# TensorE's code as one loop over two buffers: keys, values and every weight in 20 rounds of the same matmuls

## The chip, the cores and the metric

The kernel runs on one core of a Trainium2 chip. The metric is the device time of one execution in microseconds (us). Before the change it is 777.16 us, the median of 3 runs (777.11 to 777.27).

## What is computed

One decode step of a gated mix of grouped-query attention and an MLP, all in float32, for B = 2 sequences of one token, D = 1024, 32 query heads, 4 key/value heads, a cache of 32768 positions with 128 numbers each, and an MLP width F = 3584:

```python
g = sigmoid((x * gate_w).sum(-1, keepdims=True))
q = (x @ wq)                                   # 32 heads x 128
a = softmax(q @ k.T * 128 ** -0.5) @ v @ wo    # 8 query heads for each key/value head
h2 = gelu(layernorm(x) @ w3) @ w4
out = g * a + (1 - g) * (x + h2)
```

The reference has a token-shift branch with w1 and w2 too. With one token each of its shifts pads the only position away, so it adds zeros, and neither kernel loads w1 or w2. Keys and values are 2 x 134 MB, wq and wo 16.8 MB each, w3 and w4 14.7 MB each: 331 MB are read once, each used for two rows (weights) or eight query rows (caches).

## The kernel before

**Buffers and loads.** Two buffers, buf0 and buf1, each 128 partitions x 16384 numbers (8 MB), take turns. All large loads are issued by SyncE (SP) on one DMA queue: wq in two loads, w3 in two, w4 in two, then for each of the 8 pairs (key/value head x sequence) two loads of keys and two of values, then wo, whose second half comes in pieces of 8, 4, 2, 1 and 1 thousand columns (`PIECES`). A load into a buffer waits until TensorE's own count (class `Line`: one counter per engine, increased by marked instructions) says that the last matmul on the buffer's former contents is done. The small operand, x and gate_w as 16 rows of 192 numbers (x16, L140), comes first, on ScalarE's queue.

**TensorE (PE).** Its program is written out in full except for one loop. All its matmuls but one (L227) go through the helper at L135, and waits of the form "a count, then subtract it" through L132 (`take`).
- L167 to L178: x16 is spread over 128 partitions by matmuls with a selection matrix (spread), then come the sums for the gate and for the layer norm, and 16 matmuls that place the residual x(1-g) in acc, the PSUM bank that adds up the output to the end.
- L185 and L186 multiply x by wq (`columns`, L148), L187 to L194 transpose the result to queries (q_t); L195 to L204 do the same for w3 and the hidden row; L205 to L210 add h times w4 to acc (`into_acc`, L161).
- L213 to L274 are a loop (`t.Fori`) over the 8 pairs, one piece of code: 64 matmuls for scores, a transpose of the maximum (mt) and its broadcast back (bp), four times 16 small transposes of the exponentials (`turn`, L236), twice 32 matmuls with values (L245), the row sums (lp), and 8 matmuls that gather the heads (op).
- L280 to L291: the eight heads' results times wo into acc, load by load and piece by piece.

The weights of a matmul here are 32 columns wide, and four matmuls with 512 columns of the buffer fill the four quarters of 32 partitions of a PSUM bank. The scores of a pair stand in four banks (sc), 128 rows that are 8 heads x 16 slices of the cache.

**VectorE (DVE) and ScalarE (ACT)** are written out for all 8 pairs. DVE takes the maximum of the scores (L419 to L422), works out the bias (L429), copies transposed exponentials back (L435, L439) and scales the result (L456); ACT takes the exponentials (L432) and shares the copies (L437, L441). DVE's last instruction copies acc to o_sb (L464), which SP stores (L502). GpSimd (POOL) only fills constants and zeros at the start (L297 to L314).

Of the kernel before, what the change touches and what calls it, by code (L numbers as in the profile page):

```python
# [10 lines left out]
ALU = mybir.AluOpType  # L11
AX = mybir.AxisListType

# [8 lines left out]
KF = F // P  # L22
C = 32
G = P // C
# [4 lines left out]
KT = KF // G  # L29
STEP = C // B  # L30
PIECES = (8, 4, 2, 1, 1)


class Line:


    def __init__(self, engine, sem):
        self.engine, self.sem, self.n, self.seen = engine, sem, 0, {}

    def wait(self, line, value):  # L40
        if self.seen.get(id(line), 0) < value:
            self.seen[id(line)] = value
            self.engine.wait_ge(line.sem, value)

    def own(self):
        self.wait(self, self.n)

    def did(self, ins, to=None):
        if to is None:
            self.n += 1  # L50
            ins.then_inc(self.sem, 1)
        else:
            ins.then_inc(to, 1)
        return self.n
# [3 lines left out]
def kernel(  # L58
# [17 lines left out]
    def psum(name):  # L76
        return ctx.enter_context(nc.psum_tensor(name, [P, 512], F32))[:, :]
# [8 lines left out]
    bufs = [sbuf("buf0", RUN), sbuf("buf1", RUN)]  # L86
    ident = sbuf("ident", P)
    ones = sbuf("ones", P)
    spread = sbuf("spread", 4 * (P + 1), 16)
    place = sbuf("place", 3 * P + 2)  # L90
    x16 = sbuf("x16", KD * KD * 3, 16)
    xs = sbuf("xs", KD * 3)
    x_pad, xn_pad, xr_pad = (sbuf(n, KD * C) for n in ("x_pad", "xn_pad", "xr_pad"))
    h_pad = sbuf("h_pad", KF * C)
    o_pad = sbuf("o_pad", HQ * C)
    q_cur = sbuf("q_cur", E * E * C)
    sel = sbuf("sel", G * REP)
    sel_all = sbuf("sel_all", REP)
    xw, xc, sq = (sbuf(n, KD * B) for n in ("xw", "xc", "sq"))
# [3 lines left out]
    row = sbuf("row", 1024)  # L103
    q_t = sbuf("q_t", HQ * B * E)
    hid, cube, inner, bent = (sbuf(n, KT * E * PAIRS) for n in ("hid", "cube", "inner", "bent"))
    mx, l4 = ([sbuf(f"{n}{i}", NI) for i in range(2)] for n in ("mx", "l4"))
    m1, l1, bias = ([sbuf(f"{n}{i}", 1) for i in range(2)] for n in ("m1", "l1", "bias"))
    m8, mb = sbuf("m8", REP, 1), sbuf("mb", P, 1)
    lsel, norm, factor = (sbuf(n, REP) for n in ("lsel", "norm", "factor"))
    p_sb = [sbuf(f"p{i}", 512) for i in range(NI)]  # L110
    p_t = [sbuf(f"pt{i}", 512) for i in range(NI)]
    pv_sb = sbuf("pv_sb", E * 512)
    o_sb = sbuf("o_sb", D // G)
    sc = [psum(f"sc{i}") for i in range(NI)]
    tr = [psum("tr0"), psum("tr1")]
    pv = psum("pv")
    acc_bank = psum("acc")
    acc = acc_bank[:, :D // G]
    compact = at(ident, 0, (STEP, PAIRS))

    with tc.tile_critical(sync_engine=mybir.EngineType.Pool, no_gpsimd_drain=True):
        new = tc.alloc_semaphore
        landed = [new("landed0"), new("landed1")]
        pieces = [landed[1]] + [new(f"piece{i}") for i in range(1, len(PIECES))]
        edge, dvp, acp = new("edge"), new("dve_to_pe"), new("act_to_pe")
        dve, act = Line(nc.vector, new("dve")), Line(nc.scalar, new("act"))
        pool, sp = Line(nc.gpsimd, new("pool")), Line(nc.sync, None)
        pe = Line(nc.tensor, new("pe"))
        v, s, t = nc.vector, nc.scalar, nc.tensor

        def take(sem, n=1):
            t.wait_ge(sem, n).then_inc(sem, -n)  # L132

        def mm(o, lhsT, rhs, start, stop):
            return t.matmul(o, lhsT, rhs, start=start, stop=stop, skip_group_check=True)  # L135

        def quarter(t_, g):
            return t_[C * g:C * g + C]

        nc.scalar.dma_start(x16, xg.rearrange("(j p) k c -> j (p k c)", j=16)).then_inc(edge, 16)  # L140


        events = {}

        def mark(name, ins):
            events[name] = pe.did(ins)

        def columns(load, pad, n, banks):  # L148
            wide = n // G
            take(landed[load % 2], 16)  # L150
            for ek in range(E * E):
                for u, bank in enumerate(banks):
                    lo, hi = u * 512, min(u * 512 + 512, wide)
                    for g in range(G):
                        start = ek * n + g * wide
                        last = mm(quarter(bank, g)[:, :hi - lo], at(pad, ((load % 2) * 4 + ek) * C, (1, C)),
                                  bufs[load % 2][:, start + lo:start + hi],
                                  load % 2 == 0 and ek == 0, load % 2 == 1 and ek == 3)
            mark(f"load{load}", last)

        def into_acc(lhsT, rows, stop=False):  # L161
            for g in range(G):
                last = mm(quarter(acc, g), lhsT, rows[:, g * (D // G):(g + 1) * (D // G)], False, stop)
            return last
# [112 lines left out]
        def at_pair(m, name):  # L277
            return events[name] + m * per_pair
# [256 lines left out]
```

## Time and profile before

| | |
|---|---|
| median of 3 runs | 777.16 us |
| the profiled execution | 777.0 us |
| its span | 775.2 us |
| TensorE busy | 424.1 us (55%) |
| VectorE busy | 71.5 us (9%) |
| ScalarE busy | 37.2 us (5%) |
| GpSimd busy | 4.1 us (1%) |
| mean granted TensorE clock | 0.771 |
| read from memory | 331.36 MB, 427 GB/s over the span |

The profile is one execution. Its span runs from the first to the last recorded event; 1.8 us of the execution lie around it. In the profile page the digits of a row such as "DMA" are the busy share of 40 equal slices of the span, in tenths. In the table of DMA queues, q1 is SP's queue with the large loads and the store, q10 ScalarE's queue with x16, and the "instruction" queues bring the engines' own code (q8 TensorE's, q14 the others'); the columns are packets, megabytes, and the time that the packets took as a share of 16 DMA engines over the stretch. A row of the list of DMA issues gives the median time from a load's issue to its landing. A row of the timeline reads: start in us, busy time, engine, line, operation, output<-inputs, shapes, the count of instructions drawn together, and in brackets the idle time before and who ended it. A row of the groups reads: shape and count | total busy us, mean ns of one | idle time before and who ended it. "PEq L132" stands for TensorE's sequencer at a `take`. A row of the windows reads: the stretch, its length, then the busy time of PE, its weight loads, DVE, ACT, POOL and SP (the last as 0), the granted TensorE clock, the share of time in which the DMA engines are busy, and GB/s.

### The profile page before, as it was taken

The page shows a single profiled execution, that of the slowest core. Times are in us where ns is not written, and L with a number is a line of the kernel's source. Part 1 is how long each engine was busy: PE and PEld are TensorE (multiplying, and loading weights), DVE is VectorE, ACT ScalarE, POOL GpSimd, SP SyncE. Part 2 cuts the span into 40 slices and gives each one's busy share as a digit, 9 for nine tenths or more (in the row PEclk, how much of TensorE's full clock was granted, in tenths as well). Part 3 has the DMA queues.
Part 4 walks back from the last instruction along what each step waited for, and adds up shares of the span by engine and source line. Part 5 has one row for each costly group of instructions (what it writes and reads, how often), then busy time and mean ns, then how long its engine had stood idle before and what let it go on. Part 6 is the DMA issues. An engine that isn't in the chain of part 4 may idle for free. (4 is left out here: it accounts for less than half of the span.)

```text
span 775.2 us, 8891 instructions
## 1 busy us (share of the span) xinstructions
PE 424.1 (55%) x4148; PEld 181.4 (23%) x4148; DVE 71.5 (9%) x203; ACT 37.2 (5%) x88; POOL 4.1 (1%) x14
## 2 busy tenths in 40 slices
PE   3454654573647354845573647354845573647355
PEld 2121231141213121412141213121412141213123
DVE  3000100020002000200020002000200020102000
ACT  1000100020002000200020002000200020002000
POOL 2000000000000000000000000000000000000000
PEclk9876666796779776867796779777867796779779
DMA  9999999999999999999999999999999999999996
GB/s 379 437 432 454 433 418 434 433 435 434 436 433 436 433 436 436 433 433 433 433 430 433 433 433 433 433 433 436 433 433 433 433 433 433 433 433 433 433 422 263
DMA packets 6397, 331.56 MB, mean 428 GB/s; under 512 B 728, under 2 KB 752, under 8 KB 1008
## 3 DMA queue, kind: packets, MB, share of 16 engines
q1 hardware_dynamic: 6352, 331.36, 99.0%
q8 instruction: 10, 0.16, 0.1%
q14 instruction: 3, 0.02, 0.0%
q10 hardware_dynamic: 32, 0.01, 0.0%
HBM read 331.36 MB, written 0.01 MB: 427 GB/s over the span
## 5 line engine op out<-in xcount | busy, mean ns | idle before, releaser
L135 PE MATMUL sc<-buf,q_cur 128*32 128x512 f32 x1024 | 147.5, 740 | 135.9 <-PEq L132 135.9
L135 PE MATMUL pv<-buf,pt 128*32 128x512 f32 x1024 | 130.5, 668 | 106.1 <-PEq L132 106.1
L135 PEld LDWEIGHTS sc<-buf,q_cur 128*32 128x32 f32 x1024 | 40.4, 133 | 236.8 <-issue 236.8
L135 PEld LDWEIGHTS pv<-buf,pt 128*32 128x32 f32 x1024 | 38.5, 121 | 185.3 <-issue 185.1
L419 DVE TENSOR_REDUCE mx<-sc 128x1 f32<-128x512 f32 x32 | 22.1, 692 | 293.4 <-PE sc L135 293.4
L432 ACT ACTIVATE p<-sc,bias 128x512 f32<-128x512 f32 x32 | 21.6, 685 | 563.0 <-DVE bias L429 563.0
L135 PE MATMUL tr<-ident,p 128*64 128x64 f32 x1024 | 42.4, 260 | 9.2 <-PEq L132 9.2
L135 PEld LDWEIGHTS tr<-ident,p 128*64 128x64 f32 x1024 | 41.5, 172 | 9.8 <-issue 9.7
L452 DVE COPY pv_sb<-pv 128x512 f32<-128x512 f32 x16 | 10.3, 686 | 164.9 <-PE pv L135 164.9
L135 PE MATMUL sc<-buf,x_pad 128*32 128x512 f32 x128 | 16.4, 670 | 15.2 <-PEq L132 15.2
L135 PE MATMUL acc<-buf,h_pad 128*32 128x256 f32 x224 | 16.9, 474 | 14.1 <-PEq L132 14.1
L135 PE MATMUL sc<-buf,xn_pad 128*32 128x384 f32 (+1 forms) x128 | 16.6, 683 | 13.7 <-PEq L132 13.7
L135 PE MATMUL tr<-sel,pv_sb 128*128 128x8 f32 x128 | 17.3, 271 | 12.0 <-PEq L132 12.0
L135 PE MATMUL acc<-buf,o_pad 128*32 128x256 f32 x256 | 17.2, 420 | 11.9 <-PEq L132 11.9
L135 PEld LDWEIGHTS tr<-sel,pv_sb 128*128 128x128 f32 x128 | 16.8, 212 | 19.0 <-issue 19.0
L135 PEld LDWEIGHTS acc<-buf,h_pad 128*32 128x32 f32 x224 | 9.3, 136 | 21.3 <-issue 18.8
L135 PEld LDWEIGHTS acc<-buf,o_pad 128*32 128x32 f32 x256 | 9.5, 120 | 19.1 <-issue 16.2
L135 PEld LDWEIGHTS sc<-buf,x_pad 128*32 128x32 f32 x128 | 5.0, 122 | 26.2 <-issue 26.2
L135 PEld LDWEIGHTS sc<-buf,xn_pad 128*32 128x32 f32 x128 | 5.2, 135 | 24.5 <-issue 24.5
L135 PE MATMUL tr<-x,spread 16*128 16x24 f32 x16 | 3.6, 384 | 8.5 <-DMA x<-xg 8.5
L447 DVE RECIPROCAL norm<-tr 128x8 f32<-128x8 f32 x8 | 1.7, 208 | 67.2 <-PE tr L135 67.2
L435 DVE COPY pt<-tr 128x512 f32<-128x512 f32 x8 | 5.5, 692 | 19.0 <-PE tr L135 19.0
(78 smaller groups left out, 98.3 us busy)
## 6 DMA issues: line engine op xcount, KB each, us to landing
buf<-w SPq DMA_DIRECT2D x4, 7168.0 KB, 25.3
buf<-wo SPq DMA_DIRECT2D x1, 4096.0 KB, 21.3
buf<-wo SPq DMA_DIRECT2D x1, 2048.0 KB, 25.9
buf<-wo SPq DMA_DIRECT2D x1, 1024.0 KB, 28.3
buf<-wo SPq DMA_DIRECT2D x2, 512.0 KB, 29.5
buf<-kt SPq DMA_DIRECT2D x16, 29.9
buf<-vt SPq DMA_DIRECT2D x16, 29.3
buf<-wq SPq DMA_DIRECT2D x2, 32.0
```

Of the source, the lines that this page charges most:

```text
L135: return t.matmul(o, lhsT, rhs, start=start, stop=stop, skip_group_check=True)
L419: dve.did(v.reduce_max(out=mx[i2][:, i:i + 1], in_=sc[i], axis=AX.X))
L432: act.did(s.activation(p_sb[i], sc[i], AF.Exp, bias=bias[i2], scale=scale, accum_out=l4[i2][:, i:i + 1]), acp)
L435: dve.did(v.tensor_copy(p_t[0], tr[0]), dvp)
L447: dve.did(v.reciprocal(norm, tr[0][:, :REP]))
L452: dve.did(v.tensor_copy(at(pv_sb, e * P, (E * P, G), (H, 2), (1, H)), at(pv, e, (P, G), (0, 2), (2, H))), dvp if e else None)
```

## The change

TensorE's whole program becomes one loop of two phases (L185), so that its longest part is written once. Phase 0 (the Else branch, L188, which stands last) is two sums for the gate and the layer norm; phase 1 is `rounds()` (L136): 20 rounds, each of which multiplies one load in buf_a and one in buf_b by 32 column blocks of weights (`sets`, L122). In a round all 32 groups of buffer x stand in two PSUM banks; a piece that only odd rounds need (the maximum, its broadcast, the row sums, the gathering of heads) stands in an `If`. What differs between wq, w3, keys, values, w4 and wo is only what DVE, ACT and POOL write into the weights wt_a and wt_b and how they read the PSUM banks. Code with registers and branches replaces written-out code on ACT, DVE and POOL too: each has its own loop over the 8 pairs (L217, L477, L268).

- **Loads.** buf_a gets wq, wq, then all keys in turn, then wo twice; buf_b gets w3, w3, the first half of w4, then all values, and at the end the second half of w4 in pieces of 6, 4, 2, 1 and 1. SP alternates between the two, and waits for one counter `go` that DVE raises (`free`) when it has seen TensorE's event.
- **x.** One load on ScalarE's queue brings x and gate_w as 2 x 64 rows of 48 numbers (x2, L195): its source pattern has an outer dimension of 2 with step 0, so both halves of the partitions get the same 64 rows. DVE picks from it what each half needs (xs), so the spreading matmuls are gone. ScalarE's sigmoid now comes ahead of its square root.
- **Scores and exponentials.** DVE copies the scores to s_sb, which frees the PSUM banks for the next round; ACT writes each block of exponentials twice, in two layouts (`spread_rows`, p_dup); TensorE turns them with eight matmuls of 128 columns by a permutation (perm) in place of 64 small transposes, twice a round in a loop (L157); DVE copies them into wt_b (`turned`). The queries and the weight rows for wo are copied into wt_a by POOL (`queries`, `heads`).
- **End.** The residual x(1-g) enters as 4 groups of columns of a constant part of buf_b in the w3 rounds. The product with wo and with the first part of w4 gathers in acc_sb on DVE (`masked`), and four matmuls add it to acc before the last piece (L172).

```diff
+def sets(x, which, event=False):
+    for n4 in which:
+        for g in range(G):
+            n, bank = n4 * G + g, n4 // 2 % 2
+            last = mm(ps[x][C * g:C * g + C, bank * 512:bank * 512 + 512],
+                      wt[x][:, n * C:n * C + C], buf[x][:, n * 512:n * 512 + 512],
+                      n4 in (0, 2), n4 in (3, 4, 5, 7))
...
+def rounds():
+    with t.Fori(0, ROUNDS) as i:
+        with t.If(i > 0):
+            sets(1, range(5, 8), True)
+            with odd(i):
...
+        take(t, landed[0], 16)
+        take(t, ready[0])
+        sets(0, range(8), True)
+        with t.If(i < ROUNDS - 1):
+            with odd(i):
...
+            with t.Fori(0, 2):
+                take(t, acp)
+                take(t, dvp)
+                for k in range(8):
+                    last = mm(tr[:, k * P:(k + 1) * P], p_dup[:, k * P:(k + 1) * P], perm)
+                last.then_inc(pd, 1)
+        take(t, landed[1], 16)
+        take(t, ready[1])
+        sets(1, range(3))
+        take(t, piece, 16)
+        sets(1, range(3, 5), True)
...
-nc.scalar.dma_start(x16, xg.rearrange("(j p) k c -> j (p k c)", j=16)).then_inc(edge, 16)
+s.dma_start(x2, bass.AP(xg.tensor, xg.offset, [[0, 2], [2 * KD * 3, H], [1, 2 * KD * 3]])
+            ).then_inc(edge, 16)
...
+with v.Fori(0, PAIRS) as m:
+    got()
+    free()
+    scores(1)
+    wait_order()
+    v.tensor_tensor(m1, mx[:, :1], mx[:, 1:], op=ALU.max).then_inc(dvp, 1)
+    keep(1)
...
-                sp.wait(pe, needs)
-            nc.sync.dma_start(bufs[i % 2][:, :n], src).then_inc(landed[i % 2], 16)
+                sy.wait_ge(go, j - 1)
+            sy.dma_start(buf[x][:, :src.shape[1]], src).then_inc(landed[x], 16)
```

TensorE's program before, from the matmuls of w4 through the loop over pairs (L213) to wo; a row is a run of like instructions as written, with the tile of the moving and of the stationary operand behind the arrow:

```order
L135 MATMUL acc<-buf,h_pad 32x256 x112
L213 UNCONDITIONAL_BRANCH
L135 MATMUL sc<-buf,q_cur 32x512 x64
L227 MATMUL tr<-ident,m 1x128
L135 MATMUL tr<-ones,mb 128x1
L135 MATMUL tr<-ident,p 64x64 x64
L135 MATMUL pv<-buf,pt 32x512 x32
L135 MATMUL tr<-lsel,ones 128x8
L135 MATMUL pv<-buf,pt 32x512 x32
L135 MATMUL tr<-sel,pv_sb 128x8 x8
L213 REGISTER_ALU
L213 COMPARE_AND_BRANCH
```

TensorE's program after, from the head of the round (L138 asks whether it is the first) through the matmuls of buf_a to those of buf_b and the branch back (L137):

```order
L138 COMPARE_AND_BRANCH
L119 MATMUL ps_b<-buf_b,wt_b 32x512 x12
L134 REGISTER_ALU
L134 COMPARE_AND_BRANCH
L119 MATMUL sm<-lsel,ones 128x8
L119 MATMUL sm<-sel_all,pv_t 128x8 x2
L140 UNCONDITIONAL_BRANCH
L119 MATMUL ps_a<-buf_a,wt_a 32x512 x32
L151 COMPARE_AND_BRANCH
```

```order
L119 MATMUL tr<-perm,p_dup 128x128 x8
L157 REGISTER_ALU
L157 COMPARE_AND_BRANCH
L151 UNCONDITIONAL_BRANCH
L119 MATMUL ps_b<-buf_b,wt_b 32x512 x20
L137 REGISTER_ALU
L137 COMPARE_AND_BRANCH
```

The keys' and the values' matmuls, which followed one another within a pair, are now two halves of a round, and the rows for wq, w3, w4 and wo have gone into the same two; as written, TensorE has 657 matmuls before and 99 after. The last of the round's matmuls on buf_b (12 of 32) stand at the head of the next round.

SP's program before, from its start (bufs are alternated; "waits pe" is the wait for TensorE's count):

```order
L475 DMA buf0<-wq 128x16384
L475 DMA buf1<-wq 128x16384
L475 DMA buf0<-w3 128x14336 [waits pe]
L475 DMA buf1<-w3 128x14336 [waits pe]
L475 DMA buf0<-w4 128x14336 [waits pe]
L475 DMA buf1<-w4 128x14336 [waits pe]
L475 DMA buf0<-kt 128x16384 [waits pe]
```

SP's program after, from its start ("waits dve_to_sp" is the wait for the counter `go`):

```order
L567 DMA buf_a<-wq 128x16384
L567 DMA buf_b<-w3 128x14336
L567 DMA buf_a<-wq 128x16384 [waits dve_to_sp]
L567 DMA buf_b<-w3 128x14336 [waits dve_to_sp]
L567 DMA buf_a<-kt 128x16384 [waits dve_to_sp]
L567 DMA buf_b<-w4 128x14336 [waits dve_to_sp]
L567 DMA buf_a<-kt 128x16384 [waits dve_to_sp]
L567 DMA buf_b<-vt 128x16384 [waits dve_to_sp]
```

Both issue two loads without a wait and every later one behind a wait. The second load is now w3's, the third is wq's second half, and the engine waited for is VectorE instead of TensorE; the number of loads and their bytes are the same.

ScalarE's program before, from its start, with the semaphores that it waits for:

```order
L140 DMA x<-xg 16x192
L140 UNCONDITIONAL_BRANCH
L355 ACT_TABLE_LOAD
L355 ACTIVATE dev<-var 128x2 [waits dve]
L357 ACT_TABLE_LOAD
L357 ACTIVATE gate<-tr 128x2 [waits pe]
```

ScalarE's program after, from its start:

```order
L195 DMA x<-xg 128x1x48
L198 ACT_TABLE_LOAD [waits dve_to_act]
L198 ACTIVATE gate<-sm 128x2
L200 ACT_TABLE_LOAD [waits dve_to_act]
L200 ACTIVATE dev<-var 128x2
```

The load of x is 128 rows of 48 numbers where it was 16 of 192, and the table loads stand behind the waits for DVE's results where they stood ahead of them.

More of the change, by code (lines that the diff above doesn't have):

```diff
@@ L12 @@
 AX = mybir.AxisListType
+POOL = mybir.EngineType.Pool
 P = 128
@@ L21 @@
 NT = 4
-KF = F // P
-C = 32
-G = P // C
 WIDE = 8192
@@ L370 @@
-        act.did(s.copy(row[:, 512:], sc[1]), acp)
-        dve.wait(pe, events["q"])
-        dve.did(v.tensor_copy(q_t, tr[1][:, :HQ * B * E]))
-        def queries(m):
-            dve.own()
-            for half, (lo, hi) in enumerate(halves):
-                for c in range(2):
-                    last = v.tensor_copy(
-                        at(q_cur, c * C + (2 * c + half) * REP, (2 * C, E), (1, REP), rows=(lo, hi)),
-                        at(q_t, m, (PAIRS, E), (E * PAIRS, REP), rows=(lo, hi)))
-                    dve.did(last, dvp if half and c else None)
```

783 lines of the change are left out of this document (414 added, 369 removed).

## The prediction

> **What bounds the kernel now.** I read the page first, then the timeline of TensorE and the DMA view of single stretches.
>
> ```profile
> span 775.2 us, 8891 instructions
> ...
> DMA  9999999999999999999999999999999999999996
> ...
> q1 hardware_dynamic: 6352, 331.36, 99.0%
> q8 instruction: 10, 0.16, 0.1%
> q14 instruction: 3, 0.02, 0.0%
> q10 hardware_dynamic: 32, 0.01, 0.0%
> ...
> buf<-kt SPq DMA_DIRECT2D x16, 29.9
> buf<-vt SPq DMA_DIRECT2D x16, 29.3
> ```
>
> The 16 DMA engines are busy from the first slice to the last. The queue q1 holds the weights and caches: 331.36 MB in 99.0% of 16 x 775.2 us is 27.0 KB per us and engine, so a row of 64 KB takes 2.43 us, and a load of 128 rows, 8 per engine, 19.4 us. A load lands 29.9 us after its issue, so it waited some 10 us in the queue: the queue never runs dry, and compute is covered by that much.
>
> The timeline shows it as a cadence. These are the starts of TensorE's work on a load (column 1; column 2 is its length), each set off by that load's landing, and the end of the program:
>
> ```profile
> 8.51 3.60 PE L135 MATMUL tr<-x,spread 16*128 16x24 f32 x16 [8.51 <-DMA x<-xg]
> ...
> 23.11 7.07 PE L135 MATMUL sc<-buf,x_pad 128*32 128x512 f32 x64 [1.92 <-PEq L132]
> ...
> 43.46 9.30 PE L135 MATMUL sc<-buf,x_pad 128*32 128x512 f32 x64 [13.28 <-PEq L132]
> ...
> 60.99 8.21 PE L135 MATMUL sc<-buf,xn_pad 128*32 128x512 f32 x64 [5.08 <-PEq L132]
> ...
> 77.78 8.36 PE L135 MATMUL sc<-buf,xn_pad 128*32 128x512 f32 x64 [8.57 <-PEq L132]
> ...
> 94.74 8.42 PE L135 MATMUL acc<-buf,h_pad 128*32 128x256 f32 x112 [5.57 <-PEq L132]
> ...
> 111.69 8.48 PE L135 MATMUL acc<-buf,h_pad 128*32 128x256 f32 x112 [8.53 <-PEq L132]
> ...
> 440.65 8.68 PE L135 MATMUL sc<-buf,q_cur 128*32 128x512 f32 x64 [5.46 <-PEq L132]
> ...
> 460.00 9.24 PE L135 MATMUL sc<-buf,q_cur 128*32 128x512 f32 x64 [10.67 <-PEq L132]
> ...
> 750.27 9.21 PE L135 MATMUL acc<-buf,o_pad 128*32 128x256 f32 x128 [7.32 <-PEq L132]
> ...
> 771.35 0.64 PE L135 MATMUL acc<-buf,o_pad 128*32 128x256 f32 x8 [0.59 <-PEq L132]
> 772.05 0.42 DVE L464 COPY o_sb<-acc 128x256 f32<-128x256 f32 x1 [28.87 <-PE acc L135]
> 772.50 0.69 SPq L502 DMA_DIRECT2D out<-o_sb  x1
> ```
>
> A full load takes 460.00 - 440.65 = 19.35 us, and the 33 from 111.69 to 750.27 take 19.35 each; w3 and w4, 7/8 as long, take 16.95. With no delay the last piece would be at 23.11 + 35 x 19.35 + 4 x 16.95 = 768.2, and 0.3 for the small pieces at the end (estimate): 768.5. It is at 771.35, so 2.9 us are lost, and the steps say where: 23.11 to 43.46 is 1.0 too long, 43.46 to 60.99 is 0.6, and 750.27 to 771.35 is 1.4. The stretches in which the code queue q8 had packets fit. Of the DMA view, 0 to 25, 25 to 120, 120 to 200 and 750 to 772 us in turn:
>
> ```profile
> q10 hardware_dynamic: 32, 0.01, 0.2%
> ...
> q8 instruction: 5, 0.08, 0.3%
> ...
> q8 instruction: 3, 0.05, 0.3%
> ...
> q8 instruction: 2, 0.03, 0.6%
> ```
>
> That is all ten; from 200 to 750, where TensorE runs its loop (L213) again and again, there is none. A packet is 16 KB and holds one engine for 0.3% of 16 x 95 us / 5 = 0.9 us (0.6% of 16 x 22 / 2 = 1.1). A landing waits for its last engine, and an engine that never idles carries its delay to the end. The last microseconds in windows (columns before the last: TensorE's clock and the DMA share) show how unevenly they finish:
>
> ```profile
> 766.00:767.00 1.00, 1.00 (x20) 0.75 (x24) 0.00 (x0) 0.00 (x0) 0.00 (x0) 1.00 0.95 377
> 767.00:768.00 1.00, 0.90 (x19) 0.32 (x8) 0.00 (x0) 0.00 (x0) 0.00 (x0) 1.00 0.81 328
> 768.00:769.00 1.00, 0.13 (x4) 0.16 (x8) 0.00 (x0) 0.00 (x0) 0.00 (x0) 1.00 0.48 197
> 769.00:770.00 1.00, 0.94 (x16) 0.34 (x11) 0.00 (x0) 0.00 (x0) 0.00 (x0) 1.00 0.13 53
> 770.00:771.00 1.00, 0.64 (x8) 0.19 (x8) 0.00 (x0) 0.00 (x0) 0.00 (x0) 1.00 0.07 29
> ```
>
> Their shares sum to 2.4 us, so the mean engine is done at 768.4, the last about 771.2.
>
> **The change part by part.** Bytes and the cadence stay, so 768.5 stays. *Code.* TensorE's 657 written matmuls needed 0.16 MB of fetched code, 245 bytes each; 99 need 24 KB, under two packets. One was there at the start (nothing was fetched before 25 us, some 50 matmuls into the program), so one fetch stays. It falls at the start, where the program jumps to its end; nothing is fetched in the last load. The one may hit the engine that ends last (1.0, the step from 23.11) or another (0): I take 0.9, so of 2.9 us 2.0 go. The other engines' three fetches of 8 KB (q14) stay as many: VectorE has as many instructions as before.
>
> *x.* 32 small packets took 0.2% of 16 x 25 us, 0.025 us each; 128 rows with their counters are some 144, 9 per engine: 0.2 us (0 to 0.4), if they spread over all engines.
>
> *The rounds.* What hides the rest is a round of two loads, 38.7 us. The durations, from the groups (mean ns behind the comma) and four rows of the timeline:
>
> ```profile
> L419 DVE TENSOR_REDUCE mx<-sc 128x1 f32<-128x512 f32 x32 | 22.1, 692 | 293.4 <-PE sc L135 293.4
> L432 ACT ACTIVATE p<-sc,bias 128x512 f32<-128x512 f32 x32 | 21.6, 685 | 563.0 <-DVE bias L429 563.0
> L435 DVE COPY pt<-tr 128x512 f32<-128x512 f32 x8 | 5.5, 692 | 19.0 <-PE tr L135 19.0
> L355 ACT ACT_TABLE_LOAD x1 | 1.3, 1283 | 1.3 <-PEq L528 1.3
> ...
> 479.35 7.07 PE L135 MATMUL pv<-buf,pt 128*32 128x512 f32 x64 [2.33 <-PEq L132]
> ...
> 432.62 2.57 PE L135 MATMUL tr<-sel,pv_sb 128*128 128x8 f32 x16 [1.50 <-PEq L132]
> ...
> 470.04 0.16 DVE L421 TENSOR_REDUCE m<-mx 128x1 f32<-128x4 f32 x1
> ...
> 471.71 0.16 DVE L429 COPY bias<-tr 128x1 f32<-128x1 f32 x1 [0.53 <-PE tr L135]
> ```
>
> In the longer (odd) round the keys land at 0, and TensorE, cold after its wait, is done at 9.3. VectorE then releases the buffer, before any other work on this result; SP, which waited for TensorE before, now waits for that, with all later loads behind it, so a VectorE that is behind would hold the DMA. At this point it has nothing else to do. The maximum over 1024 columns takes two of the 0.69 (10.7), the steps from it to the bias 1.8 as now, plus 1.4 for the copy of the scores that stands between them on VectorE (13.9). Two exponentials take 1.4 (15.5 with the hand-over). Eight matmuls with 128 weight columns took 2.57 at 8 moving columns; 128 moving columns add up to 7.07 / 8 / 4 = 0.22 each where nothing overlaps, so 2.6 to 4.4 (18 to 20). Then 1.4 for the next exponentials, beside VectorE's two copies of the first block, the second eight matmuls, and two copies: the weights for the values stand at 24 to 27. The values landed at 19.35. Their 32 matmuls come warm, 7.07: the buffer is free at 31 to 34. It has to be by 38.7 less 1 us of start-up (the first issue at 0.9, data from about 1.9) and 2 us by which the first engines lead, 35.5. The even round lacks the maximum and the bias. GpSimd's eight copies of the next queries start at VectorE's second copy of the scores (15) and are wanted with the next keys at 38.7; no row shows such a copy, but they fit up to 2.9 us each. I count 0 for the rounds; if this cover goes, the third rival has the price.
>
> *End.* Before the last piece, VectorE adds two PSUM halves (1.4 us) and TensorE four matmuls (0.6) more; the pieces before it leave some 5 us after the piece that starts this. I take 0.1 (0 to 0.5).
>
> The sum: -2.9 + 0.9 + 0.2 + 0.1 = -1.7. The profiled execution took 777.0 (its span and 1.8 around it), 0.16 less than the median, so the median 777.16 becomes 775.5. All lag gone, and nothing added, gives 774.3; all upper ends, 776.5.
>
> **The rivals.** *x comes too late* (slower). The x load is 128 rows of 192 bytes whose source pattern has an outer dimension of 2 with step 0. x landed at 8.5 us before, issued at 0.9, with one row and one counter per engine: about one wait of 2.43 us for each, behind q1's rows. One row per turn on 16 engines lands x at about 26, and the first multiplication ends near 39.5 instead of 30, about when the two loads under way run out (23.1 + 16.95 = 40): 0 to 1.5 us. But if the outer 2 splits the load over two engines only, each has 64 rows; 16 go between the rows of the two loads, the others after these end, so x lands at about 44. The statistics take 4.6 (3.3 as in the rows below, and a table load of 1.28 that now stands behind a wait), the multiplication 9.3 and the start of the third load 1: data again at 59 instead of 40. That is 19 us: 794. It decides from x at about 26 on. For it: nothing else in this program loads with such a pattern; against it: no trace here shows small rows taking one turn each, or two engines.
>
> ```profile
> 12.15 0.39 DVE L333 COPY xs<-tr 64x24 f32<-64x24 f32 x2 [6.56 <-PE tr L135]
> ...
> 15.46 0.16 DVE L353 TENSOR_SCALAR var<-tr 128x2 f32<-128x2 f32 x1 [0.74 <-PE tr L135]
> ```
>
> [...]
>
> *Code is fetched again in each round.* 20 fetches over 16 engines, one or two each, delay the last by 1.0 to 2.9: the gain shrinks to 0 to 1.9, 776.8. [...] Eight passes over 203 matmuls, 50 KB by the above, and no packet from 200 to 750 speak against it.
>
> *The odd rounds are late* (slower). If the buffer of values is free 1 us after its limit in each of 8 pairs, that costs 8 us, 785; it takes all of 4 us more than I count, such as TensorE at half clock through both groups.
>
> **How the numbers follow.** The forecast has 0.50, x late by a gap 0.30, code fetched again 0.14, odd rounds late 0.06. A measurement of this kernel can tell about 0.2% (1.55 us) from no change: 775.6 is the border, and my 775.5 lies just beyond it. Of the forecast 0.34 falls below, of the second rival 0.04: faster 0.38. Same has 0.16 and 0.10: 0.26. Slower is 0.36. The forecast's own range is 774.3 to 776.5; with the gap in, 774.3 to 796.
>
> **What would show it.** Right: q8 with one or two packets, none after 100 us; last piece about 1.7 us earlier; DMA slices full. Wrong: DMA share under 0.9 between 39 and 60 us and the first multiplication after 40 us (x), q8 packets in each round (code), a step over 19.5 us in mid-kernel (rounds).

## The result, and the profile after

The changed kernel takes 796.31 us (median of 6 runs, 793.34 to 797.26), the kernel before 777.12 (6 runs, 776.82 to 777.27): a ratio of 1.0243, interval 1.0226 to 1.0260, slower by 2.4%. The forecast was 775.5. The median lies 0.3 above the upper end of the range, which had been set by the first rival, x that comes too late. The profiled execution took 796.0, its span 794.2.

The page of after: the span, the busy share of the DMA engines in 40 slices of 19.9 us, and the queues.

```profile
span 794.2 us, 8176 instructions
...
DMA  9919999999999999999999999999999999999997
...
q1 hardware_dynamic: 6352, 331.36, 96.9%
q10 hardware_dynamic: 130, 0.02, 0.0%
q14 instruction: 3, 0.02, 0.0%
q8 instruction: 1, 0.02, 0.0%
```

One slice is nearly empty, the third, 40 to 60 us. The load of x (q10) made 130 packets: 128 rows of 192 bytes and 2 of 4 bytes, called counters here. Before, it was 32, 16 rows and 16 counters, and each of the 44 large loads has 16 counters beside its 128 rows, as many as there are engines; so now two engines carried x, with 64 rows each. Its rows came two at a time, at 7.61 and 7.68 us, 10.03 and 10.10, 12.46 and 12.53. TensorE's code came in one packet (q8) where it was ten. The code did what was expected of it.

The timeline of after, from the arrival of x to the first release of a buffer:

```profile
40.20 0.71 DVE L322 COPY xs<-x 64x12 f32<-64x12 f32 x4 [30.67 <-DMA x<-xg]
...
41.64 0.56 PE L119 MATMUL sm<-part,ones 128*128 128x4 f32 x2 [41.64 <-PEq L116]
...
42.63 1.28 ACT L198 ACT_TABLE_LOAD   x1 [42.63 <-ACTq L116]
...
45.84 9.50 PE L119 MATMUL ps_a<-buf_a,wt_a 128*32 128x512 f32 x64 [0.88 <-PEq L116]
...
55.55 0.33 SPq L567 DMA_DIRECT2D buf_a<-wq  x1
```

x is there at 40.2, when the two loads under way are just ending. Of the DMA view, 0 to 39 and 39 to 42 us in turn show how it came:

```profile
q10 hardware_dynamic: 30, 0.01, 0.1%
...
q10 hardware_dynamic: 100, 0.02, 3.1%
```

In 39 us the two engines brought 30 of x's packets, about one each for every large row; the other 100 packets passed within 0.7 us (39.2 to 39.9), when the large rows had ended. Then the statistics take 5.6 us, the product 9.5, and SP can issue the third load at 55.55. The DMA engines had nothing to move meanwhile. In windows (the last two columns are the DMA share and GB/s; a packet counts where it starts, and the 0.17 is the first rows of the third load, which start from 56.5 on):

```profile
20.00:38.70 18.70, 0.00 (x0) 0.00 (x0) 0.00 (x0) 0.00 (x0) 0.00 (x0) 1.00 0.92 400
38.70:57.30 18.60, 11.36 (x74) 4.33 (x75) 4.25 (x21) 2.94 (x4) 0.32 (x2) 1.00 0.17 57
```

The product that the third load sets off, the second on buf_a, starts at 78.21. The rest of the loss is spread over the rounds. The timeline of after again: this start, the start of the product on buf_a in the first round with values, an odd round from 461.82 with what follows in it, the starts of the next two rounds, and the start of the last round. (A count below x64 means that the view ended within the product. To release a buffer means here that SP issues the next load into it.)

```profile
78.21 8.68 PE L119 MATMUL ps_a<-buf_a,wt_a 128*32 128x512 f32 x64 [8.20 <-PEq L116]
...
150.81 9.49 PE L119 MATMUL ps_a<-buf_a,wt_a 128*32 128x512 f32 x60 [6.39 <-PEq L116]
...
461.82 9.72 PE L119 MATMUL ps_a<-buf_a,wt_a 128*32 128x512 f32 x64 [5.47 <-PEq L116]
...
477.88 3.44 PE L119 MATMUL tr<-perm,p_dup 128*128 128x128 f32 x16 [2.24 <-PEq L116]
...
483.39 2.94 PE L119 MATMUL tr<-perm,p_dup 128*128 128x128 f32 x16 [2.06 <-PEq L116]
...
488.11 8.53 PE L119 MATMUL ps_b<-buf_b,wt_b 128*32 128x512 f32 x64 [1.78 <-PEq L116]
...
496.85 0.33 SPq L567 DMA_DIRECT2D buf_b<-vt  x1
...
500.54 8.77 PE L119 MATMUL ps_a<-buf_a,wt_a 128*32 128x512 f32 x64 [3.90 <-PEq L116]
...
540.95 9.41 PE L119 MATMUL ps_a<-buf_a,wt_a 128*32 128x512 f32 x64 [5.80 <-PEq L116]
...
773.17 9.35 PE L119 MATMUL ps_a<-buf_a,wt_a 128*32 128x512 f32 x64 [5.89 <-PEq L116]
```

In the odd round that begins at 461.8 the buffer of values is released at 496.85, 35.0 after the keys' product began and 3.7 before the product on the next load of keys. The product that follows the one at 500.54 begins at 540.95: 40.41 us later, where two loads need 38.70. From 150.81 to 773.17, 16 rounds, the products on buf_a advance by 622.4, not by 16 x 38.70 = 619.2: 3.2 us lost.

### The profile page after: what moved, and what is told of

It is laid out like the page before. It is cut to its first block, busy times and chain, and to the rows that moved or that the text cites. A ratio compares the mean times of both kernels' runs of the same rounds, so it can differ in the third digit from the quotient of the medians.

```text
span 794.2 us, 8176 instructions
## 1 busy us (share of the span) xinstructions
PE 472.9 (60%) x3275; PEld 213.5 (27%) x3275; DVE 159.5 (20%) x326; ACT 54.5 (7%) x106; POOL 22.2 (3%) x93
## 5 line engine op out<-in xcount | busy, mean ns | idle before, releaser
L119 PE MATMUL ps_a<-buf_a,wt_a 128*32 128x512 f32 x1280 | 184.7, 742 | 105.2 <-PEq L116 105.2
L119 PE MATMUL ps_b<-buf_b,wt_b 128*32 128x512 f32 x1256 | 163.2, 678 | 45.8 <-PEq L116 45.7
L119 PE MATMUL tr<-perm,p_dup 128*128 128x128 f32 x608 | 103.9, 342 | 60.3 <-PEq L116 60.3
L119 PEld LDWEIGHTS tr<-perm,p_dup 128*128 128x128 f32 x608 | 96.4, 249 | 72.9 <-issue 72.9
L119 PEld LDWEIGHTS ps_a<-buf_a,wt_a 128*32 128x32 f32 x1280 | 52.6, 132 | 228.4 <-issue 228.4
L119 PEld LDWEIGHTS ps_b<-buf_b,wt_b 128*32 128x32 f32 x1256 | 47.9, 123 | 148.3 <-issue 148.1
L208 ACT ACTIVATE p_dup<-s_sb,bias 128x512 f32<-128x512 f32 x64 | 47.5, 744 | 570.6 <-ACTq L116 570.6
L418 DVE TENSOR_REDUCE mx<-ps_a 128x1 f32<-128x1024 f32 x17 | 20.8, 1225 | 234.0 <-DVEq L116 234.0
L473 DVE COPY wt_b<-tr 64x512 f32<-64x512 f32 x64 | 44.1, 689 | 104.5 <-DVEq L116 103.1
L421 DVE COPY s_sb<-ps_a 128x1024 f32<-128x1024 f32 x17 | 20.7, 1217 | 0.0
```

The lines of the kernel that those rows point to most:

```text
L208: last = s.activation(at(p_dup, d * H, (512, 2), (P, 4), (1, H)), at(src, bank * 512, (1, 2), (P, 4), (2, H)), func, **more)
L418: v.reduce_max(out=mx[:, L:L + 1], in_=ps[0], axis=AX.X)
L421: v.tensor_copy(s_sb[:, L * 1024:(L + 1) * 1024], ps[0]).then_inc(dp, 1)
L473: last = v.tensor_copy(at(wt[1], b * H, (P, 8), (1, H), rows=(lo, hi)), at(tr, tau * H, (P, 8), (1, H), rows=(lo, hi)))
```

## The experiments

Twelve kernels were run. Each number is a median; "before" is the kernel before on the same chip, 776.8 to 776.95. The experiments on x come first, then those on the odd rounds, then those on the code.

**x in two loads (e1_x_two_loads).**

```diff
-s.dma_start(x2, bass.AP(xg.tensor, xg.offset, [[0, 2], [2 * KD * 3, H], [1, 2 * KD * 3]])
-            ).then_inc(edge, 16)
+for lo, hi in halves:
+    s.dma_start(x2[lo:hi], bass.AP(xg.tensor, xg.offset, [[2 * KD * 3, H], [1, 2 * KD * 3]])
+                ).then_inc(edge, 16)
```

> The changed kernel, but x comes in two loads of 64 rows, one for each half of the partitions, without the outer dimension of step 0. Theory (the single load of 128 rows was carried by two DMA engines, 64 rows each: 130 packets in the profile of after are 128 rows and 2 counters; each row waited for one 64 KB row of the weights): 128 rows and 32 counters, 160 packets on q10, 4 rows and a counter per engine and load; x lands after some 10 turns, at 20 to 26 us instead of 40.1; no slice with DMA under 0.9 before 60 us; of the 17.6 us of idle DMA at least 16.5 go. What is left is 796.3 - 17.6 = 778.7, less or more by the odd rounds, whose losses (about 3 us in the profile of after) may fall otherwise: 776 to 779.5. Rival (small rows wait one turn each whatever the engines, and x is late by its 128 rows): x still lands at 35 or later, 790 or more. Rival (x is not the cause, the first product is late through ScalarE's table loads and code): x lands early, but the first product starts after 40 and the time stays over 790.

784.07 us, ratio 1.0091 (1.0076 to 1.0106). The page and the timeline:

```profile
DMA  9979999999999999999999999999999999999997
...
q10 hardware_dynamic: 160, 0.02, 0.0%
```

```profile
28.36 0.71 DVE L323 COPY xs<-x 64x12 f32<-64x12 f32 x4 [18.83 <-DMA x<-xg]
...
43.59 0.33 SPq L568 DMA_DIRECT2D buf_a<-wq  x1
```

All 16 engines carry x (160 = 128 + 2 x 16), and it comes 12 us earlier. 12.2 us are gained, not 16.5: x was expected by 26 and came at 28.4, and 43.59 is still too late. Each engine had ten small packets, four rows and a counter twice. By the packets' records the first of them start at 7.4, behind two large rows, from then on each engine takes one for each large row, and the last starts at 27.9. Spreading over engines is most of it, but the number of rows for each engine counts too.

**The load of x added to the kernel before (b1_before_x2, b2_before_x2_two).**

```diff
+nc.scalar.dma_start(x2, bass.AP(xg.tensor, xg.offset, [[0, 2], [2 * KD * 3, H], [1, 2 * KD * 3]])).then_inc(edge, 16)
...
-t.wait_ge(edge, 16)
+t.wait_ge(edge, 32)
```

In b2 it is the two loads of e1 instead, and the wait is for 48.

> The kernel before, with the changed kernel's load of x (128 rows, outer dimension 2 of step 0) added behind its own on the same queue, and TensorE's first matmul waiting for both; nothing reads the added rows. Theory (this form of load alone makes x late): the added load lands at about 40, the statistics and the first product follow, 8.5 to 23 in the profile of before being the time that they and the first landing took, so the product starts at about 46 to 48 and the DMA stands still for 16 to 21 us: 793 to 798. Rival (the loss needs the changed kernel's loop, table loads or order): 777 to 779.

> The kernel before, with the same 128 rows added, but as two loads of 64 rows; TensorE waits for both. Theory: the added rows land at 22 to 28 us on 16 engines, 10 to 12 packets for each; the first product starts at 29 to 37 instead of 23.1 and its end still comes at about the moment when the two loads under way run out, so 777 to 781. Rival (rows wait one turn each whatever the engines): as with the single load, 793 or more.

800.09 us, ratio 1.0299 (1.0284 to 1.0315), and 788.36 us, ratio 1.0148 (1.0133 to 1.0164). Both are beyond what was expected, by 2 and by 7, since the kernel before does more between x and the end of its first product (in b1 20.0 us from x at 42.71 to the issue of the third load at 62.73; in after 15.4). The page of each (b1, then b2):

```profile
DMA  9908999999999999999999999999999999999996
...
q10 hardware_dynamic: 162, 0.04, 0.0%
```

```profile
DMA  9949999999999999999999999999999999999996
...
q10 hardware_dynamic: 192, 0.04, 0.0%
```

The single load costs 23 us and two loads cost 11 in a kernel that has none of the other changes: the form of the load is enough. 162 is 16 + 16 for x16 and 128 + 2 for the single load; 192 is 32 and 160.

**x as before, spread by matmuls (e7_x16).** The changed kernel with the load of x16 and eight spreading matmuls in phase 0.

```diff
-s.dma_start(x2, bass.AP(xg.tensor, xg.offset, [[0, 2], [2 * KD * 3, H], [1, 2 * KD * 3]])
+s.dma_start(x16, xg.rearrange("(j p) k c -> j (p k c)", j=16)).then_inc(edge, 16)
...
+t.wait_ge(edge, 16)
+for e in range(E):
+    for w in range(4):
+        last = mm(tr[:, e * 24:e * 24 + 24], spread[:, w * P:(w + 1) * P],
+                  x16[:, (2 * w + e) * 24:(2 * w + e) * 24 + 24], w == 0, w == 3)
```

> The changed kernel with x loaded as the kernel before does it: 16 rows of 192 numbers, one row and one counter for each DMA engine, spread over the partitions by eight matmuls (written into phase 0). Theory (x waits one turn of the 64 KB rows for each of its rows and counters on an engine: 2 turns landed it at 8.5 us, 10 turns at 28.4, and 64 rows on two engines at 40.1): x lands at 8 to 9, the first product starts with the landing of wq at 22 to 24, no idle DMA before 60 us; 5.4 us less than the run with two loads of x: 777.5 to 779.5, the rest above the blind forecast being odd rounds that are late. Rival (with x early enough the change gives what was forecast): 774.3 to 776.5. Rival (something else in the start is late too: table loads behind waits, the code of phase 1): idle DMA of more than 1 us before 60.

779.71 us (8 runs, 777.84 to 782.70), ratio 1.0035 (1.0023 to 1.0047). The DMA view of its first 42 us gives the time from the issue of x to its landing; the first product, in the timeline, starts with the landing of wq:

```profile
x<-xg ACTq DMA_DIRECT2D x1, 12.0 KB, 8.7
```

```profile
24.42 9.04 PE L120 MATMUL ps_a<-buf_a,wt_a 128*32 128x512 f32 x64 [5.55 <-PEq L117]
...
60.72 9.66 PE L120 MATMUL ps_a<-buf_a,wt_a 128*32 128x512 f32 x64 [7.59 <-PEq L117]
```

The gap is gone; the third load's product starts at 60.72, in after at 78.21: 17.5 us for x. x is there at 9.6 with two packets on each engine (8.5 in before), at 28.4 with ten (e1) and at 40.2 with 64 rows and more on two engines: a dose and its answer. What is left, 779.71, is still slower than before, and 0.2 above what was expected.

**Odd rounds made shorter or longer (e8_x16_keep, e9_x16_later, e12_one_pdup_half).** All on e7. In e8 VectorE copies the scores (`keep`) after the bias. In e9 it makes two extra copies in the odd round. e12 is e8, and the maximum over the first bank of scores is taken while TensorE fills the second; its spreading is four matmuls of 48 columns.

```diff
-            keep(1)
             got()
             v.reduce_max(out=m8, in_=sm[:1, MT:MT + P].rearrange("p (s h) -> p h s", h=REP), axis=AX.X)
...
             v.sem_inc(dvp, 1)
+            keep(1)
```

```diff
+            v.tensor_copy(slow, s_sb[:, :1024])
+            v.drain()
+            v.tensor_copy(slow, s_sb[:, :1024])
+            v.drain()
             turned(1, ready[1])
```

```diff
                 if x == 0 and n4 == 5:
+                    last.then_inc(ph, 1)
...
+            take(v, ph, 2)
+            v.reduce_max(out=mx[:, 1:2], in_=ps[0][:, :512], axis=AX.X)
             got()
             free()
-            scores(1)
+            v.reduce_max(out=mx[:, 2:3], in_=ps[0][:, 512:], axis=AX.X)
```

> As the run with 16 rows of x, and in odd rounds VectorE copies the second half of the scores (1.22 us) after the bias instead of ahead of it. Theory (odd rounds are at the limit: in the profile of after the buffer of values came free 3.0 to 5.2 us before the landing of the keys' load that was under way, and steps grew where this was under some 3.4): the bias comes 0.5 to 1.2 us earlier, so the margin is 3.6 to 6.2 and steps over 19.5 us on the last engine go, but for one of code: 0.5 to 2 us less than without the move. Rival (long steps are the DMA's own): no change by the move.

> As the run with 16 rows of x, with two copies of 1024 columns by VectorE added in each odd round between the second turning and the copies of the weights for the values; nothing reads what they write. Theory (a buffer of values that is late costs its lateness in each pair): 2.4 to 2.6 us later, of which the margin above 3.4 (0 to 1.8, mean 0.8) hides a part: 8 times 1 to 2, 8 to 16 us more than without them. Rival (the queue covers it, or long steps are the DMA's own): under 3 us more.

> The same without the two buffers for the exponentials (the turning matmuls stay a loop of two). Theory: 0.6 us for the maximum and up to 0.6 for the copy off the chain of odd rounds, buffers free at 33 to 34.7; part of the pairs still late: 776.5 to 779. Rival (TensorE slower): as the run with the copy moved, 779 to 780.

e8: 779.40 us (775.92 to 781.93), ratio 1.0028 (1.0016 to 1.0040), no different from e7 by these intervals, where 0.5 to 2 less were expected. e9: 784.40, ratio 1.0106 (1.0092 to 1.0121), 4.7 more than e7 where 8 to 16 were expected. e12: 775.93 (11 runs, 775.66 to 776.26), ratio 0.9988 (0.9979 to 0.9997), 3.8 less than e7 and below the 776.5 to 779 that were expected: a version that beats the kernel before, but by 0.1% only, with an interval that ends just below 1. So VectorE's added copies cost time and its earlier maximum saves some, but not in proportion. The rows say why. In e7, the odd round whose keys' product starts at 603.70, in windows (the product on keys, the two turns, the product on values; PEclk is the third number from the end):

```profile
603.70:613.20 9.50, 9.50 (x64) 2.57 (x64) 0.00 (x0) 0.00 (x0) 0.00 (x0) 0.74 0.99 428
619.55:622.95 3.40, 3.35 (x16) 3.16 (x16) 0.00 (x0) 0.00 (x0) 0.00 (x0) 0.59 1.34 578
624.96:628.10 3.14, 3.03 (x16) 2.74 (x16) 0.00 (x0) 0.00 (x0) 0.00 (x0) 0.63 0.91 397
629.77:638.30 8.53, 8.44 (x64) 2.35 (x64) 0.00 (x0) 0.00 (x0) 0.00 (x0) 0.84 0.91 392
```

The kernel before, the values of its pair at 479.35:

```profile
479.35:486.50 7.15, 7.15 (x66) 2.50 (x66) 0.00 (x0) 0.00 (x0) 0.00 (x0) 1.00 0.99 431
```

The values' product took 8.44 at a clock of 0.84, not 7.07 at 1.00, and the release came at 638.42, 34.7 after the start of the keys' product. So it was in four of e7's eight odd rounds; in the other four the product took 7.07 but began 0.5 to 1.5 us later, and the release came 33.9 to 34.4 after the start. e12 and e8 in their odd rounds at the same place of the program (the values' product, the release, the next keys; e12 first):

```profile
622.35 8.63 PE L121 MATMUL ps_b<-buf_b,wt_b 128*32 128x512 f32 x64 [1.78 <-PEq L118]
631.19 0.33 SPq L582 DMA_DIRECT2D buf_b<-vt  x1
...
637.15 8.04 PE L121 MATMUL ps_a<-buf_a,wt_a 128*32 128x512 f32 x48 [6.17 <-PEq L118]
```

```profile
628.56 8.87 PE L120 MATMUL ps_b<-buf_b,wt_b 128*32 128x512 f32 x64 [1.78 <-PEq L117]
637.64 0.33 SPq L576 DMA_DIRECT2D buf_b<-vt  x1
```

In e12 the release leads the next keys by 6.0 us, in e7 by 4.1 (638.42 to 642.47). In e8 the bias came at 616.28, 13.5 after its product began at 602.74 (13.8 in e7), yet the first turn took 3.75 (3.40 in e7), the values 8.87, and the release stands 34.9 after the start: what VectorE gave, a slower TensorE took. In all eight odd rounds of e8 the values' product took 8.6 to 8.9. Over the 16 rounds the products on buf_a lose 7.1 us in e7 (133.30 to 759.62) and 0.85 in e12 (133.21 to 753.26; e7 first):

```profile
133.30 9.21 PE L120 MATMUL ps_a<-buf_a,wt_a 128*32 128x512 f32 x64 [5.76 <-PEq L117]
...
759.62 8.37 PE L120 MATMUL ps_a<-buf_a,wt_a 128*32 128x512 f32 x64 [4.74 <-PEq L117]
```

```profile
133.21 9.14 PE L121 MATMUL ps_a<-buf_a,wt_a 128*32 128x512 f32 x64 [5.84 <-PEq L118]
...
753.26 7.15 PE L121 MATMUL ps_a<-buf_a,wt_a 128*32 128x512 f32 x40 [5.36 <-PEq L118]
```

The profiled executions of e7 and e8 are their slowest (782.70 and 781.93), so the 7.1 us are more than the medians show. In e9 the release is 36.2 to 37.2 after the start of the keys' product in every pair, and each pair loses 0.7 to 1.4 us: late by more than that, but the DMA queue bears a part.

The counters tell why the same release costs time in one round and none in another. The eight profiles with this loop and its odd rounds (after, e1, e3, e7, e8, e9, e11, e12) have 64 odd rounds. Where the first of the 16 engines still had 2.5 us or more of the keys' load to move when the buffer of values was released (28 rounds), the first counter of the values' load came 19.34 us after the first of the keys' load, to within 0.1, but for two rounds with 0.3 more. Where it had 1.55 us or less left (29 rounds), it came 0.3 to 1.8 us later than that: the first engines had run dry. (The seven rounds between: 0 to 0.3.) The first engine led the last by 1.2 to 2.3 us in after's odd rounds and by 1.9 to 3.0 in e7's, so e7 lost more with releases that were no later.

**Two buffers for the exponentials (e3_two_pdup on e1, e11_all on e12).** TensorE's loop of two turns is written out, with a buffer of its own for each.

```diff
-                    with t.Fori(0, 2):
+                    for pb in p_dup:
                         take(t, acp)
                         take(t, dvp)
                         for k in range(8):
-                            last = mm(tr[:, k * P:(k + 1) * P], p_dup[:, k * P:(k + 1) * P], perm)
+                            last = mm(tr[:, k * P:(k + 1) * P], pb[:, k * P:(k + 1) * P], perm)
```

> As the run with x in two loads, and ScalarE's doubled exponentials have two buffers, so that the second block of a round doesn't wait for TensorE to have turned the first; TensorE's eight turning matmuls are written out twice instead of looped. Theory (in odd rounds the buffer of values comes free 33.5 to 35.7 us after the keys have landed, the later end being past what the DMA queue can bear): this takes 1.5 us or more from the chain, the values' buffer is free at 32 to 34.3, no step between landings on the last engine over 19.5 us, and the time is that of the blind forecast, 774.3 to 776.0, some 2 us under the run with x in two loads alone. Rival (the steps that are too long come from the DMA engines themselves, not from late buffers): the same time as the run with x in two loads, and long steps stay. Rival (less code brings nothing): 777 or more with no long steps.

> The changed kernel with 16 rows of x (spread by four matmuls of 48 columns), two buffers for ScalarE's exponentials with the turning matmuls written out twice, the copy of the scores behind the bias, and the maximum over the first PSUM bank of scores taken while TensorE still fills the second. Theory (x and the odd rounds are all that stands between the changed kernel and the blind forecast): x in time, buffers of values free 2 us or more earlier than with 16 rows of x alone (31.5 to 33.5 us after the keys land instead of 34.2 to 35.2), no idle DMA between 5 and 760 us but a few tenths, last engine at 770 to 771.5: 774.5 to 776.5. Rival (earlier work only meets a slower TensorE, as the move of the copy did: 0.3 us gained for 0.55 moved): 778 to 780 and buffers free at 34 or later. Rival (code written out again brings fetches that cost what was gained): more than five packets of TensorE's code, 776.5 to 778.

In both, the queries are turned from a buffer that holds zeros (in e3 the MLP's hidden row too); transfers and instructions are those of the others. e3: 782.96 us, ratio 1.0079 (1.0065 to 1.0092), 1.1 less than e1 (the intervals overlap) and not 2, and far above 776, since e1's gap at the start was still in it, which the expectation forgot. e11: 775.88 (11 runs, two of them at 777.5 and 778.0), ratio 0.9992 (0.9983 to 1.0001): with x early and odd rounds short the time is in the forecast's own range. Its releases come 29.7 to 31.6 after the start of the keys' product, and every round with values takes 38.7 to 38.9 us. It has five packets of TensorE's code where e12 has one, and is no faster.

**Code alone (b3_less_wo, b4_less_wo_w4).** The kernel before with fewer written matmuls.

```diff
-for eh in range(E * REP):
+for eh in range(E * REP - 1, E * REP):
```

b4 has the same cut in the loop over w4.

> The kernel before without 60 of the 64 matmuls on the first load of wo (15 of 32 heads' share of the product with wo is left out of the output); loads are as they were. It is there for the code: 60 written matmuls less, some 15 KB, so one packet of TensorE's code less at the end. Theory (each packet delays one DMA engine by some 1.0 to 1.5 us for good, and at the end that is the engine that lands last): last landing 0.4 to 1.5 us earlier, 775.6 to 776.6. Rival (code packets cost nothing that shows): 776.8 to 777.2.

> As the run with less of wo, and also without 104 of the 112 matmuls on w4 (13 of 14 blocks of each half of the hidden row are left out of the output): some 41 KB of code less, 7 packets instead of 10. Theory: the packets left fall on other engines; the last engine's delay over the first is 1.8 to 3.2 us instead of 3.6: 775.2 to 776.8, not more than the run with less of wo by over 0.5. Rival: 776.8 to 777.2.

b3: 776.70 us, ratio 0.9998 (0.9989 to 1.0007): no difference, where 776.6 at most was expected. b4: 775.86, ratio 0.9988 (0.9979 to 0.9998). Their code queues (b3 first, then b4):

```profile
q8 instruction: 9, 0.15, 0.1%
```

```profile
q8 instruction: 7, 0.11, 0.1%
```

One packet less brings nothing, three less bring 1 us. From 750 us to the last landing the kernel before has two packets of code, at 755.3 and 765.2, b3 has one, at 764.2, and b4 none. The counters that end the last load show what each did: in before 14 engines are done by 769.54 and two at 770.35 and 770.79, in b3 15 by 769.61 and one at 770.74, in b4 all by 769.29. So what counted here was not the number of packets but whether one fell into the last loads: in b3 the one that was left made its engine as late as before.

**A loop longer than the code that was fetched (e10_x16_far).** On e7, with 70 small matmuls that only round 0 executes.

```diff
+                with t.If(i < 1):
+                    for k in range(70):
+                        mm(ps[1][:, :REP], ones, ones[:, :REP])
```

> As the run with 16 rows of x, with 70 small matmuls (a product of ones that nothing reads) in the loop of rounds in a branch that only round 0 takes: the loop grows by the code of some 18 KB, and 19 rounds jump over it. Theory (code that lies within what TensorE holds is not fetched again, code beyond it is): fetches on TensorE's code queue in each round, 20 to 60 in all; each delays one of 16 engines by about 1.0 to 1.5 us (16 KB at 29.3 us of before: 1.00, and 0.46 more on the next row), so the last engine is 2 to 5 us later, 1 to 4 us more than without them. Rival (a far jump stalls TensorE too, so that rounds are late): more than 6 us. Rival (no fetch in the rounds): one or two packets more, and within 1 us of the run without them.

804.00 us, ratio 1.0339 (1.0324 to 1.0353). The time says nothing of code: the 70 matmuls themselves took 30 us in round 0, and the first product waited for them.

```profile
23.81 30.03 PE L120 MATMUL ps_b<-ones 128*128 128x8 f32 x140 [0.82 <-issue]
53.77 8.75 PE L120 MATMUL ps_a<-buf_a,wt_a 128*32 128x512 f32 x64
```

But its page has six packets of TensorE's code in the whole run, five of them before 58 us: at most one in the 19 rounds that jump over 70 matmuls, 17 KB at 245 bytes each (estimate), where 20 to 60 were expected. That code is fetched in each round was not shown.

```profile
q8 instruction: 6, 0.10, 0.0%
```

## Why the prediction was wrong, step by step

- **What bounds the kernel, and the cadence: right.** Two loads take 38.70 us in every round that isn't late, in all kernels. The time is the DMA's, plus what makes it wait.
- **x: the step that failed.** The prediction counted 9 packets for each engine and 0.2 us, "if they spread over all engines", and gave the other case, two engines, a chance of 0.30 as a rival. It was the other case: 130 packets. The rival's price was 19 us and its x at 44; measured were 17.5 and 40.2, because the 100 packets that were left when the two loads ended took 0.7 us; the statistics took 5.6 where 4.6 were counted. The runs show the split by their counts: 130 packets here and 162 in b1 for the single load, 160 and 192 for two loads of 64 rows. No row on record before the run showed how such a load is shared out; both 16 engines and two, and the chance of 0.30, were the author's estimate.
- **That 16 engines would do: wrong too.** The prediction had x at 26 on 16 engines and 0 to 1.5 us of loss; e1 had 28.4, started the second product on buf_a at 66.34 where e7 did at 60.72, and took 4.4 us more than e7. That small rows take one turn each behind 64 KB rows, which no row before the run had shown, is now shown by 9.6, 28.4 and the two packets for each turn in after (7.61 and 7.68, then 10.03 and 10.10).
- **The rounds: wrong by a little, at a place without room.** "I count 0" failed: 3.8 us between e7 and e12. The count to the weights, 24 to 27 us, was right (25.7 to 27.2 in e7). The release was counted at 31 to 34 and came at 33.9 to 34.9 in e7, 33.2 to 35.4 in after. In half of these rounds "their 32 matmuls come warm, 7.07" failed: they took 8.4 to 8.7. In the other half they took 7.07, and the weights came at the late end of the count. But no release passed the limit of 35.5 (by its own terms, 38.7 less 1 and 2, it is 35.7), so the limit was too wide as well. The product starts some 0.7 us after the last engine's counter, which was left out; the first engine leads by up to 3.0 us, not 2; and the start-up takes more than 1 us: in after the issue at 55.55 set the 16 engines going between 56.50 and 57.28, and their first rows took 3.0 us in place of 2.43. By the 64 odd rounds the first engine needs about 2.5 us left. The third rival named the mechanism with a chance of 0.06, and thought that it took 4 us more than counted; a release some 2 us past the middle of the count was enough.
- **Code: one packet, as forecast, but half the gain.** Ten packets became one, and none after the first in the last load. But e12, where little else is left, gains 0.9 us and not 1.7: its last piece starts at 770.28 against 771.35, and the forecast had 769.65. What is shown to have cost time in before are the two packets in the last loads (770.79 against b4's 769.29); early packets cost little, since e11 has four in its first 35 us, e12 one, and their times are the same (775.88 and 775.93). An early delay did stay: in before, after two packets (29.35 and 58.74 us), the last counter of a load came 2.2 us behind the first at 77 us and still at 750. The rounds of e12 lost 0.85: a step of 39.0 and one of 39.2 where 38.7 were due. The first falls together with a packet of the other engines' code (q14) at 207 us, as do the steps beside such a packet in after (227 us, 8 KB, 0.33 us), e1 (216) and e3 (213), though in after a late buffer falls there too; the prediction left these packets out because their number stays. The second follows e12's latest release, 34.0 after the start of the keys' product.
- **Code fetched again in each round: no**, as forecast. After had one packet in 20 rounds, at 7.5 us; its loop has 77 matmuls, 19 KB at 245 bytes each (estimate). e10, whose loop has 36 KB by the same estimate, had six in all and at most one after 58 us.
- **The end: right.** The last piece of after starts 0.8 before VectorE's copy of acc (790.21, 791.01), in before 0.7 (771.35, 772.05), and in all three kernels, e12 too, the last piece starts 0.5 to 0.6 us after the last engine's counter.

The sum of after, by the last piece: 771.35, and -1.1 for all that e12 shows, 17.6 for x (78.21 against e12's 60.63) and 2.3 for the rounds (3.2 less e12's 0.85), makes 790.2; measured 790.21. What stays open: why TensorE's clock is below 1.00 in the values' product of half the odd rounds of after, e7 and e12 and of all in e8 and e9. It has more waits between its matmuls there (2.21, 2.06 and 1.78 us) than the kernel before; that these cause it was not tried. In e3 and e11, with two buffers for the exponentials, the product took 7.07 in all eight.

## What to carry to other kernels

In a kernel that the DMA bounds, look first at what the very first product waits for: here 24 KB of input, with 64 rows on each of two engines, queued behind the large rows, and the whole pipe started 17.5 us late. Read the packet count of a small load (rows plus counters) in the profile: here 2 counters went with two engines (130 packets) and 32 with two loads on all 16 (160). And when a change takes the slack out of a round, compare the release of each buffer with the landing that is under way, with TensorE at the clock that it has (here 8.44 us at 0.84), not at its best (7.07 at 1.00).

## What the runs showed of the hardware that was not expected

- A load of 128 rows whose source has an outer dimension of 2 with step 0 was carried by two DMA engines (after: 130 packets, 2 of them counters); as two loads of 64 rows it was carried by 16 (e1: 160 packets, 32 of them counters).
- Beside rows of 56 and 64 KB, each small row or counter of another queue took one turn of an engine, 2.1 to 2.4 us in after: two of them on each engine landed at 8.5 us in before and 9.6 in e7, ten at 28.4 in e1. Without large rows, 100 of them on two engines passed in 0.7 us (after, 39.2 to 39.9).
- With one packet of 16 KB of code in the last loads, which took 1.1 us on its engine, that engine ended 1.1 us after all others (b3, 770.74 and 769.61); four early packets in place of one made no difference in time (e11, 775.88, and e12, 775.93).
- A loop of TensorE's with 147 written matmuls, 36 KB at 245 bytes each (estimate), and a jump over 70 of them in it, had six packets of code in the whole run (e10), at most one of them after 58 us.
